# Reordering a linear-attention plus gated-MLP kernel behind its first gate block, with one batch's key features in 32-token tiles and one copy on ScalarE

## The chip, the cores and the metric

The kernel runs on one core of one Trainium2 chip. The metric is the device time of one execution in microseconds (us), the median over the runs shown; lower is better. The core has a matrix engine (TensorE, PE in the profile; its weight loads are shown apart as PEld), a vector engine (VectorE, DVE), an activation engine (ScalarE, ACT), a general engine (GpSimd, POOL) and a sync engine (SyncE, SP), which here only starts transfers (DMA). Each engine runs its own instructions strictly in the order in which the program wrote them.

## The reference

Four batches, four heads, 1088 tokens, 32 features a head. Queries and keys go through two 8x32 projections whose outer product gives 64 features; the attention is linear in them; its result x (1088 x 128 per batch) goes through a gated MLP in which the tokens are mixed by a 1088 x 1088 matrix:

```python
def phi(x):
    a = np.einsum('rd,bhsd->bhsr', S1, x)
    b = np.einsum('rd,bhsd->bhsr', S2, x)
    return np.einsum('bhsi,bhsj->bhsij', a, b).reshape(*x.shape[:-1], r * r)
q_p, k_p = (phi(q), phi(k))
kv = np.einsum('bhsf,bhsd->bhfd', k_p, v)
z = np.sum(k_p, axis=2)
num = np.einsum('bhsf,bhfd->bhsd', q_p, kv)
den = np.einsum('bhsf,bhf->bhs', q_p, z)[..., None] + 1e-06
...
h = gelu_tanh(x @ w_in)
u, v = (h[..., :d_ff // 2], h[..., d_ff // 2:])
v_n = (v - mean(v)) / np.sqrt(var(v) + 1e-06) * g_ln
v_s = np.einsum('ts,bsd->btd', w_sg, v_n) + b_sg[None, :, None]
gated = u * v_s
return (x + gated @ w_out)
```

Here d_ff is 1024, so v_n is 1088 x 512 for each batch, and the product with w_sg is the bulk of the work.

## The kernel before

Every large product keeps fp32 accuracy by splitting each operand into a high and a low part (`_h`, `_l`) and adding three products: high by high, high by low, low by high. In the token mixing these are the matmuls of lines 851 (`z_hi`, two a tile) and 860 (`z_lo`).

The 1088 tokens are cut into 9 tiles of 128 (the last half full) where they are contracted, and into three chunks of 362, 362 and 364 columns where they are the output. The 512 channels of v are four blocks of 128 (`db`). For each batch the stages are:

- `k1` (line 404): the keys of each token tile times the projections, into the PSUM tiles `pk`; `kb` (line 416, ScalarE) copies half of that; `features` (line 211, VectorE) makes the 64 products per head, `kp`; `k2` (line 436) contracts `kp` with v and a column of ones over the tokens, into `pkv`: 4 matmuls of 32 rows for each tile and pair of heads. `kv` (lines 447 and 448) copies `pkv` into `kv`, the second copy broadcasting the denominator's column to 32 columns.
- the same features for the queries (`qt`, `pab`, `ab`, `e_..`, `qph`, `qpl`: lines 469 to 529; they go through DRAM to be spread over partitions), then numerator and denominator (`pnd`, `den`), giving x and its split `x_h`, `x_l`.
- `unit`: `pu` (lines 875 to 877), three matmuls per block and chunk, then gelu on ScalarE, `u` (line 882). `pv` (lines 746 to 755), gelu `vn` (760), the layer norm's statistics (776 to 828), its split `vh` (838, ScalarE) and `vl` (843, VectorE).
- the token mixing `pz` (lines 851, 860) and then on VectorE `gt` = pz times gain plus bias (`scale`, line 888), times u (`gate`, line 895), split into `gh` (900, ScalarE) and `gl` (903, VectorE), and the output product `po` (lines 921 to 924), whose sum with x is stored.

PSUM has 8 banks, and every `pz`, `pu`, `po`, `pk`, `pkv` and so on takes the next of them (`bank`), so a matmul group that opens a bank waits until the last reader of that bank's earlier tile is done. Weights and inputs come by DMA; `w_l` are the low parts of w_sg, made on VectorE during batch 0.

Batch 3 does the mixing in another way (class `Fast`): sums of blocks of w_sg (`t1` to `t4`) are built in DRAM by transfers that GpSimd starts, loaded by `high` (line 1103, GpSimd's queue, into `wt_..h`) and by `load` (line 1096, SyncE, into `wr`), and `low` (line 1107, VectorE) subtracts to get `wt_..l`; the products are then those of lines 1012 to 1019, with tiles named `pz_(0, 'v')` and the like, and lines 1046 and 1050 for the third chunk.

The order of all this is written out by hand. Each piece is registered as a step by `at`, and a table `WHEN` of 1773 numbers gives each step its place; `Steps.run` sorts by it and emits the steps in that order, so the table sets the order on all engines at once:

```python
def run(self, tc):
    when = WHEN or range(len(self.steps))
    with tc.manual_schedule():
        for i in sorted(range(len(self.steps)), key=lambda i: (when[i], i)):
            self.steps[i][1]()
```

Of the kernel before, what the change touches and what calls it, by code (L numbers as in the profile page):

```python
# [15 lines left out]
B, H, S, D, R = 4, 4, 1088, 32, 8  # L16
P = 128
# [13 lines left out]
NARROW = 9  # L31
# [121 lines left out]
def tile_kernel(tc, qd, kd, vd, sd, wd, bd, wind, woutd, q0d, vid, outd, pool, dram, psum):  # L153
    nc = tc.nc
    mm = nc.tensor.matmul
    V, A, G = nc.vector, nc.scalar, nc.gpsimd
# [12 lines left out]
    T = {}  # L169
# [220 lines left out]
    class Attention:  # L390
# [9 lines left out]
        def k1(self, pk, t, i):  # L400
            k = T[f"k{self.b}"]
# [1017 lines left out]
```

## Time and profile before

| | |
|---|---|
| time, median of 3 runs (lowest to highest) | 322.85 us (322.66 to 323.17) |
| the profiled execution: its time / its span | 322.65 us / 320.9 us |
| TensorE busy, of the span | 312.4 us (97%) |
| VectorE busy | 273.2 us (85%) |
| ScalarE busy | 161.7 us (50%) |
| GpSimd busy | 35.0 us (11%) |
| mean granted TensorE clock | 0.997 |

The profile is of one execution. Its span runs from the first to the last instruction; 1.75 us of the execution's own time lie around it. A matmul record overlaps the next, so a matmul of 362 columns is shown with 0.32 us while a new one starts every 0.16 us; a loss on PE is therefore read from the starts.

### The profile page before, as it was taken

Reading aid. Unit: us, or ns where it says so; the run is one execution under the profiler, and the core shown is the slowest. Engines: PE = TensorE matmul, PEld = TensorE weight load, DVE = VectorE, ACT = ScalarE, POOL = GpSimd, SP = SyncE. Lnnn points to the kernel's source line nnn. Section 1 sums busy time; section 2 is a strip of 40 time slices with the busy share of each in tenths; the row PEclk is TensorE's granted clock in tenths of the full one; section 3 lists DMA queues with packets and bytes.
Section 4 is the critical chain, followed back from the end, with each engine's and each line's share of the span. In section 5 each row is a group of like instructions: output and inputs, shape, how many; then the busy total and the mean of one; then the engine's idle time right before and its main releaser. Section 6 shows DMA issues by size and latency. Waiting matters only on the chain.

```text
span 320.9 us, 6477 instructions
## 1 busy us (share of the span) xinstructions
PE 312.4 (97%) x2474; PEld 298.7 (93%) x2474; DVE 273.2 (85%) x660; ACT 161.7 (50%) x354; POOL 35.0 (11%) x52
## 2 busy tenths in 40 slices
PE   8999999899999999999999998999999999999995
PEld 6777999799999999999999997999999999999995
DVE  5999999999998968597988875598997889889865
ACT  4689814646549825354537930446345762433411
POOL 0300000024301100203400000333010000000000
PEclk9999999999999999999999999999999999999998
DMA  7999934764468625735160005684160022400002
GB/s 227 368 429 361 400 152 135 186 175 132 188 98 198 123 57 143 192 100 176 12 113 24 2 29 119 162 221 136 25 194 24 0 76 33 162 23 1 2 0 69
DMA packets 19774, 42.27 MB, mean 132 GB/s; under 512 B 2176, under 2 KB 14624, under 8 KB 19328
## 3 DMA queue, kind: packets, MB, share of 16 engines
q1 hardware_dynamic: 14784, 27.17, 27.5%
q0 software_dynamic: 4960, 14.70, 17.3%
q8 instruction: 19, 0.31, 0.4%
q14 instruction: 11, 0.09, 0.1%
HBM read 35.87 MB, written 8.94 MB: 140 GB/s over the span
## 4 chain that ended last, share of the span: by engine, by line
PE 79%; DVE 14%; issue 2%; ACT 2%; DMA 1%; SPq 1%; DVEq 0%; ACTq 0%
PE pz L851 28%; PE pz L860 12%; PE pz L1050 5%; DVE w_l L719 2%; PE pu L875 2%; PE pu L877 2%; PE pu L876 2%; PE pv L746 2%; PE pv L747 2%; PE pv L755 2%; PE po L924 2%; PE po L922 2%; PE po L921 2%; DMA vn<-in_q 1%; PE pkv L436 1%
## 5 line engine op out<-in xcount | busy, mean ns | idle before, releaser
L851 PE MATMUL pz<-w_h,vh 128*128 128x362 f32 (+1 forms) x324 | 105.4, 326 | 0.8 <-ACT u L882 0.8
L851 PE MATMUL pz<-w_h,vl 128*128 128x362 f32 (+1 forms) x324 | 105.2, 325 | 0.4 <-DVE vl L843 0.4
L860 PE MATMUL pz<-w_l,vh 128*128 128x362 f32 (+1 forms) x288 | 87.0, 324 | 0.0
L851 PEld LDWEIGHTS pz<-w_h,vh 128*128 128x128 f32 x324 | 60.8, 188 | 1.9 <-ACT u L882 1.1
L851 PEld LDWEIGHTS pz<-w_h,vl 128*128 128x128 f32 x324 | 60.8, 188 | 1.6 <-DVE vl L843 0.9
L860 PEld LDWEIGHTS pz<-w_l,vh 128*128 128x128 f32 x288 | 53.1, 188 | 0.1
L882 ACT ACTIVATE u<-pu 128x362 f32<-128x362 f32 (+1 forms) x48 | 22.6, 473 | 28.5 <-DVE gt L895 15.4
L900 ACT CAST gh<-gt 128x362 fp32r<-128x362 f32 (+1 forms) x47 | 22.7, 492 | 18.6 <-DVE gt L895 15.9
L888 DVE SCALAR_TENSOR_TENSOR gt<-pz,vi,b_bc 128x362 f32<-128x362 f32 (+3 forms) x41 | 23.6, 579 | 7.1 <-PE pz L851 6.3
L828 ACT ACTIVATE vn<-vn,nm,rs 128x512 f32<-128x512 f32 x36 | 28.1, 812 | 2.9 <-DVE nm L822 2.1
L903 DVE TENSOR_TENSOR gl<-gt,gh 128x362 fp32r<-128x362 f32 (+1 forms) x47 | 25.4, 547 | 2.6 <-ACT gh L900 2.0
L760 ACT ACTIVATE vn<-pv 128x512 f32<-128x512 f32 x36 | 21.0, 598 | 11.8 <-PE pv L755 11.0
L895 DVE TENSOR_TENSOR gt<-gt,u 128x362 f32<-128x362 f32 (+3 forms) x49 | 25.5, 525 | 0.8 <-ACT u L882 0.3
L776 DVE BATCH_NORM_STATS2 st<-vn 128x6 f32<-128x512 f32 x33 | 22.5, 683 | 3.9 <-ACT vn L760 3.2
L843 DVE TENSOR_TENSOR vl<-vn,vh 128x128 fp32r<-128x128 f32 (+1 forms) x54 | 22.2, 428 | 1.9 <-ACT vh L838 1.7
L550 DVE RECIPROCAL den<-den 128x362 f32<-128x362 f32 (+1 forms) x9 | 21.7, 2415 | 1.3 <-ACT den L545 1.2
L838 ACT CAST vh<-vn 128x128 fp32r<-128x128 f32 (+1 forms) x54 | 19.6, 403 | 6.2 <-PE pz L851 5.8
L1050 PE MATMUL pz<-w_h,wb 128*128 128x364 f32 x64 | 18.8, 324 | 0.0
L529 POOL TENSOR_TENSOR qpl<-e_0a,qph 128x362 fp32r<-128x362 f32 x6 | 6.3, 1056 | 109.9 <-ACT qph L524 83.9
L875 PE MATMUL pu<-x_h,win_h 128*128 128x362 f32 (+1 forms) x48 | 16.2, 337 | 0.0
L545 ACT ACTIVATE den<-pnd,mask 64x362 f32<-64x362 f32 (+1 forms) x18 | 10.1, 560 | 11.4 <-PE pnd L538 11.3
L876 PE MATMUL pu<-x_h,win_l 128*128 128x362 f32 (+1 forms) x48 | 15.7, 328 | 0.0
(330 smaller groups left out, 635.7 us busy)
## 6 DMA issues: line engine op xcount, KB each, us to landing
w_f<-in_w SPq DMA_DIRECT2D x9, 576.0 KB
wt<-in_w POOLq DMA_DIRECT2D x6, 768.0 KB, 7.7
w_h<-in_w POOLq DMA_DIRECT2D x2, 1152.0 KB, 8.5
vi<-in_v SPq DMA_DIRECT2D x7, 306.0 KB
w_h<-in_w POOLq DMA_DIRECT2D x1, 1728.0 KB, 14.5
k<-in_k SPq DMA_DIRECT2D x3, 576.0 KB
wt<-wt POOLq DMA_DIRECT2D x2, 768.0 KB, 6.8
out<-o SPq DMA_DIRECT2D x8, 181.0 KB
```

Source lines behind the costliest of these rows:

```text
L776: V.bn_stats(st, self.vn[:, t])
L828: A.activation(self.vn[:, t], self.vn[:, t], AF.Identity, bias=self.nm[:, t : t + 1], scale=self.rs[:, t : t + 1])
L843: V.tensor_sub(vl[:, ts], self.vn[:, ts, P * db : P * db + P], f32(vh[:, ts]))
L851: mm(self.z[db, ci], lhsT=self.parts[db][i][:, t], rhs=T["w_h"][:, t, AT[ci] : AT[ci] + cw], start=(t == 0 and i == 0), stop=(t == NT - 1 ...
L860: mm(self.z[db, ci], lhsT=self.parts[db][0][:, t], rhs=T["w_l", t][:, AT[ci] : AT[ci] + CH[ci][1]], start=False, stop=False,)
L875: mm(pu, lhsT=T["win_h"][:, ws], rhs=xh[:, cs], start=True, stop=False)
L882: A.activation(self.u[db, ci], self.pu.pop((db, ci)), AF.Gelu_apprx_tanh)
L888: V.scalar_tensor_tensor(self.gt[db, ci][:, s], self.z[db, ci][:, s], T["g_col"][:, db : db + 1], T["b_bc"][:, c0 : c0 + cw][:, s], op0=AL ...
L895: V.tensor_mul(gt, gt, self.u[db, ci][:, s])
L900: A.copy(self.g[db, ci][0], self.gt[db, ci])
L903: V.tensor_sub(self.g[db, ci][1], self.gt.pop((db, ci)), f32(self.g[db, ci][0]))
L1050: mm(self.z[db, ci], lhsT=w[:, i, t % 4], rhs=r[:, cs], start=(t == 0 and q == 0), stop=False)
```

## The change

The order of the first 339 steps, up to the end of batch 0's first gate block (about 46.7 us in the trace of before), stays. Behind it nearly every number of `WHEN` is new. Three more edits:

- `k1` works in tiles of 32 tokens instead of 64 for batch 1 (`D` is 32), so its 18 matmuls become 36 with half the output rows; the trace shows each fp32 matmul as two records. Batches 0, 2 and 3 stay.
- The copy of the denominators in `kv` (line 448) is issued on ScalarE instead of VectorE, in all batches, 2 a batch.
- `NARROW` goes; since it was 9 and t is below 9, `n` in `k2` is what it was.

```diff
-NARROW = 9
...
-    282, 284, 287, 291, 296, 293, 299, 304, 301, 309, 365, 103, 105, 109, 118, 130, 116, 137, 115, 142, 145, 153,
-    157, 166, 173, 182, 187, 192, 198, 201, 180, 275, 286, 360, 319, 328, 368, 371, 367, 223, 230, 264, 272, 305,
+    282, 284, 287, 291, 296, 293, 299, 304, 301, 309, 358, 103, 105, 109, 118, 130, 116, 137, 115, 142, 145, 153,
+    157, 166, 173, 182, 187, 192, 198, 201, 180, 275, 286, 360, 319, 328, 371, 485, 378, 223, 230, 264, 272, 305,
...
-            for r in range(0, P, 64):
+            n = D if self.b == 1 else 2 * D
+            for r in range(0, P, n):
                 mm(
-                    self.pk[t][r : r + 64], lhsT=k[:, P * t + r : P * t + r + 64], rhs=T["sk"][:, :64],
+                    self.pk[t][r : r + n], lhsT=k[:, P * t + r : P * t + r + n], rhs=T["sk"][:, :64],
                     start=True, stop=True, skip_group_check=True,
                 )
...
-            n = D if self.b or t >= NARROW else 2 * D
+            n = D if self.b else 2 * D
...
-                    V.tensor_copy(self.kvf[r, 1:3, c], self.pkv[r, :, D : D + 1].broadcast_to([64, 2, D]))
+                    A.copy(self.kvf[r, 1:3, c], self.pkv[r, :, D : D + 1].broadcast_to([64, 2, D]))
```

What the new numbers do is read from the instructions on each engine. A row is line, operation, out<-in and the shape; `pu_2_0` is block 2, chunk 0, and the last number of a name only counts tiles.

**TensorE, batch 0 and the k2 of batch 1, before.** The two units and the first mixing of block 2 (rows 245 to 253 of 1718; the k2 of batch 1 is in rows 233 to 235):

```order
L875 MATMUL pu_2_0_1014<-x_h,win_h 128x362
L876 MATMUL pu_2_0_1014<-x_h,win_l 128x362
L877 MATMUL pu_2_0_1014<-x_l,win_h 128x362
L875 MATMUL pu_2_1_1027<-x_h,win_h 128x362
L876 MATMUL pu_2_1_1027<-x_h,win_l 128x362
L877 MATMUL pu_2_1_1027<-x_l,win_h 128x362
L851 MATMUL pz_2_0_1034<-w_h,vh_2_885 128x362
L851 MATMUL pz_2_0_1034<-w_h,vl_2_886 128x362
L860 MATMUL pz_2_0_1034<-w_l_709,vh_2_885 128x362
```

**The same engine, after.** The units, the k2 (L436) and the first mixing of block 2 (rows 233 to 244 of 1719):

```order
L875 MATMUL pu_2_0_913<-x_h,win_h 128x362
L876 MATMUL pu_2_0_913<-x_h,win_l 128x362
L877 MATMUL pu_2_0_913<-x_l,win_h 128x362
L875 MATMUL pu_3_0_918<-x_h,win_h 128x362
L876 MATMUL pu_3_0_918<-x_h,win_l 128x362
L877 MATMUL pu_3_0_918<-x_l,win_h 128x362
L436 MATMUL pkv_927<-vi,kp_0_885 32x34 x24
L436 MATMUL pkv_927<-vi,kp_1_899 32x34 x24
L436 MATMUL pkv_927<-vi,kp_2_907 32x34 x24
L851 MATMUL pz_2_0_1002<-w_h,vh_2_814 128x362
L851 MATMUL pz_2_0_1002<-w_h,vl_2_815 128x362
L860 MATMUL pz_2_0_1002<-w_l_709,vh_2_814 128x362
```

The k2 of batch 1 has moved from in front of these units and of the six `po` matmuls between to a place directly ahead of the mixing of block 2, with a unit of block 3 ahead of it.

**TensorE, the k2 of batch 2, before.** What stands between the k1 of batch 2 (rows 596 and 597) and its k2; the last 9 rows and the k2 (rows 606 to 617):

```order
L921 MATMUL po_1_1804<-gh_0_1_1702,wout_h 128x362
L922 MATMUL po_1_1804<-gh_0_1_1702,wout_l 128x362
L924 MATMUL po_1_1804<-gl_0_1_1703,wout_h 128x362
L851 MATMUL pz_1_0_1720<-w_h,vh_1_1610 128x362
L851 MATMUL pz_1_0_1720<-w_h,vl_1_1611 128x362
L860 MATMUL pz_1_0_1720<-w_l_646,vh_1_1610 128x362
L851 MATMUL pz_1_0_1720<-w_h,vh_1_1610 128x362
L851 MATMUL pz_1_0_1720<-w_h,vl_1_1611 128x362
L860 MATMUL pz_1_0_1720<-w_l_666,vh_1_1610 128x362
L436 MATMUL pkv_1825<-vi,kp_0_1792 32x34 x24
L436 MATMUL pkv_1825<-vi,kp_1_1808 32x34 x24
L436 MATMUL pkv_1825<-vi,kp_2_1818 32x34 x24
```

**The same place, after.** The last 9 rows ahead of the k2, and the k2 (rows 565 to 576; its k1 is in rows 519 and 520):

```order
L860 MATMUL pz_0_0_1519<-w_l_735,vh_0_1478 128x362
L479 MATMUL pab_1_1719<-qt_1h,sk_76 128x362
L480 MATMUL pab_1_1719<-qt_1l,sk_75 128x362
L851 MATMUL pz_0_1_1598<-w_h,vh_0_1478 128x362
L851 MATMUL pz_0_1_1598<-w_h,vl_0_1479 128x362
L860 MATMUL pz_0_1_1598<-w_l_679,vh_0_1478 128x362
L851 MATMUL pz_0_0_1519<-w_h,vh_0_1478 128x362
L851 MATMUL pz_0_0_1519<-w_h,vl_0_1479 128x362
L860 MATMUL pz_0_0_1519<-w_l_679,vh_0_1478 128x362
L436 MATMUL pkv_1742<-vi,kp_0_1726 32x34 x24
L436 MATMUL pkv_1742<-vi,kp_1_1738 32x34 x24
L436 MATMUL pkv_1742<-vi,kp_2_1681 32x34 x24
```

Between the k1 and the k2 of batch 2 there were 17 matmuls, and there are 53 now. For batch 3 the k2 moves from row 1013 to row 939, which with the repeats in the rows and the weight loads makes about 77 fewer TensorE instructions ahead of it.

**VectorE, near the end, before.** The last low part of batch 3's weights, `wt_1l` (L1107), and the rows ahead of it (rows 554 to 565 of 624; the L1107 ahead of it is row 550):

```order
L895 TENSOR_TENSOR gt_0_0_3677<-gt_0_0_3677,u_0_0_3544 128x362
L979 TENSOR_TENSOR wb_0s_3699<-vn_3180,wb_0s_3699 128x512
L913 TENSOR_TENSOR x_f_3711<-x_h,x_l 128x364
L994 TENSOR_TENSOR vn_3180<-vn_3180 128x4x128
L888 SCALAR_TENSOR_TENSOR gt_0_2_3726<-pz_0_2_3466,vi,b_bc 128x364
L941 TENSOR_TENSOR o_2_3629<-o_2_3629,x_l 128x364
L903 TENSOR_TENSOR gl_0_0_3722<-gt_0_0_3677,gh_0_0_3721 128x362
L895 TENSOR_TENSOR gt_0_2_3726<-gt_0_2_3726,u_0_2_3731 128x364
L979 TENSOR_TENSOR wb_13_3751<-vn_3180,wb_13_3751 128x512
L986 TENSOR_TENSOR we_2_3705<-vn_3180,we_2_3705 128x128
L941 TENSOR_TENSOR o_1_3613<-o_1_3613,x_l 128x362
L1107 TENSOR_TENSOR wt_1l<-wr_3724,wt_1h 128x3x362
```

**The same place, after.** From the L1107 whose end frees the buffer `wr` of the load (rows 556 to 567 of 623):

```order
L1107 TENSOR_TENSOR wt_0l<-wr_3580,wt_0h 128x362
L1107 TENSOR_TENSOR wt_0l<-wr_3580,wt_0h 128x2x362
L1036 SCALAR_TENSOR_TENSOR vi<-pz_(0, 'w')_3619,vi 128x362
L895 TENSOR_TENSOR gt_2_2_3733<-gt_2_2_3733,u_2_2_3698 128x364
L908 TENSOR_TENSOR wout_f<-wout_h,wout_l 128x128
L1036 SCALAR_TENSOR_TENSOR gt_0_0_3789<-pz_(0, 'x')_3449,vi,b_bc 128x362
L979 TENSOR_TENSOR wb_0s_3752<-vn_3180,wb_0s_3752 128x512
L903 TENSOR_TENSOR gl_2_2_3784<-gt_2_2_3733,gh_2_2_3783 128x364
L1036 SCALAR_TENSOR_TENSOR gt_0_1_3797<-pz_(0, 'u')_3724,vi 128x362
L913 TENSOR_TENSOR x_f_3805<-x_h,x_l 128x362
L941 TENSOR_TENSOR o_2_3690<-o_2_3690,x_l 128x364
L1107 TENSOR_TENSOR wt_1l<-wr_3770,wt_1h 128x3x362
```

The two last L1107 stood 15 rows apart (rows 550 and 565) and now stand 10 apart (rows 557 and 567).

## Rows read from the trace of the kernel before

**Rows 1.** The page: busy time of each engine, and the chain by engine.
```profile
PE 312.4 (97%) x2474; PEld 298.7 (93%) x2474; DVE 273.2 (85%) x660; ACT 161.7 (50%) x354; POOL 35.0 (11%) x52
...
PE 79%; DVE 14%; issue 2%; ACT 2%; DMA 1%; SPq 1%; DVEq 0%; ACTq 0%
```

**Rows 2.** Windows: us, then busy us (instructions) of each engine, clock, DMA.
```profile
50.00:60.00 10.00, 9.62 (x221) 8.77 (x220) 9.81 (x24) 7.47 (x18) 0.00 (x0) 1.00 0.70 198
60.00:70.00 10.00, 9.22 (x53) 8.27 (x52) 9.83 (x24) 3.94 (x9) 1.68 (x2) 1.00 0.66 181
...
190.00:200.00 10.00, 8.57 (x215) 8.08 (x215) 6.12 (x18) 1.50 (x5) 0.00 (x0) 1.00 0.46 94
```

**Rows 3.** Waits of PE: engine line <- releaser: us, times, longest.
```profile
PE pkv L436 <- issue: 1.4, 1, 1.4
...
PE pz L851 <- ACT u L882: 0.8, 1, 0.8
...
PE pkv L436 <- ACT u L882: 0.4, 1, 0.4
```

**Rows 4.** Timeline of PE, 53 to 64 us: start, us, engine, line, operation [idle <-releaser].
```profile
53.43 1.27 PE L404 MATMUL pk<-sk,k 128*64 128x64 f32 x36
54.63 0.43 PE L875 MATMUL pu<-x_h,win_h 128*128 128x362 f32 x1
...
57.73 1.49 PE L436 MATMUL pkv<-vi,kp 128*32 128x34 f32 x144 [0.37 <-ACT u L882]
...
61.86 0.32 PE L877 MATMUL pu<-x_l,win_h 128*128 128x362 f32 x1
62.96 0.43 PE L851 MATMUL pz<-w_h,vh 128*128 128x362 f32 x1 [0.78 <-ACT u L882]
63.23 0.33 PE L851 MATMUL pz<-w_h,vl 128*128 128x362 f32 x1
```

**Rows 5.** Timeline of VectorE, 55 to 62 us.
```profile
55.50 3.06 DVE L211 TENSOR_TENSOR kp<-pk,kb 128x256 f32<-128x256 f32 x9
...
61.81 0.53 DVE L895 TENSOR_TENSOR gt<-gt,u 128x364 f32<-128x364 f32 x1
```

**Rows 6.** Timeline of ScalarE, 62 to 63 us.
```profile
62.43 0.47 ACT L882 ACTIVATE u<-pu 128x364 f32<-128x364 f32 x1 [2.72 <-DVE gt L895]
```

**Rows 7.** Timeline of PE, 125 to 128 us.
```profile
125.70 1.95 PE L436 MATMUL pkv<-vi,kp 128*32 128x34 f32 x144
```

**Rows 8.** Line 436: records with ns min/median/max, and the idle time before them.
```profile
L436 PE MATMUL pkv<-vi,vn x72: 224/224/245, 10.7 to 12.8; 128*64 128x34 f32 x72
...
  DVE kp L211: 0.2, 1
```

**Rows 9.** Timeline of PE, 194 to 198 us.
```profile
194.86 1.42 PE L436 MATMUL pkv<-vi,kp 128*32 128x34 f32 x136
197.71 0.27 PE L436 MATMUL pkv<-vi,kp 128*32 128x34 f32 x8 [1.43 <-issue]
```

**Rows 10.** Instruction queue in the page's part 3: packets, MB, share of 16 engines.
```profile
q8 instruction: 19, 0.31, 0.4%
```

**Rows 11.** The same queue between 195.2 and 196.5 us.
```profile
q8 instruction: 1, 0.02, 4.5%
```

**Rows 12.** Groups by line and shape: busy us, mean ns | idle before.
```profile
L448 DVE COPY kv<-pkv 64x64 f32<-64x64 f32 x6 | 1.3, 213 | 0.0
```

**Rows 13.** The same of ScalarE, its smallest copies.
```profile
L416 ACT COPY kb<-pk 128x32 f32<-128x32 f32 x3 | 0.6, 188 | 0.4 <-PE pk L404 0.4
```

**Rows 14.** Timeline of SyncE's queue, near 272 us.
```profile
272.17 0.32 SPq L1096 DMA_DIRECT2D wr<-wt  x1
```

**Rows 15.** Timeline of VectorE, near 281 us.
```profile
281.28 1.29 DVE L1107 TENSOR_TENSOR wt_1l<-wr,wt_1h 128x1086 fp32r<-128x1086 f32 x1
```

**Rows 16.** Timeline of PE, near 284 us.
```profile
283.83 0.32 PE L1013 MATMUL pz_(0, 'v')_3774<-wt_1l,wb 128*128 128x362 f32 x1
```

**Rows 17.** DMA issues between 270 and 282 us: KB, us to landing.
```profile
wt_1h<-wt POOLq DMA_DIRECT2D x1, 576.0 KB, 4.5
```

150 rows, old and new, of the table WHEN are left out of this document.

## The prediction

> **What bounds the kernel now.** I read the busy times and the chain first: TensorE is busy 312.4 of 320.9 us, and the chain that ended last is 79% PE [rows 1]. VectorE at 85% is next, but it waits for PE as often as PE for it. So the kernel is bound by TensorE's own instructions, and a new order that keeps all of them can only win what PE loses between them: 320.9 - 312.4 = 8.5 us at the most, of which the start and the tail, where the order stays or nearly stays, hold a large part. The granted clock is 1.00 (the 2.4 GHz level) in each of the windows [rows 2], so there is nothing to win in clock.
>
> Next come the windows of 10 us behind the point from which the order is new. Nearly all have PE at 10.00. Three do not: 9.62 at 50 to 60 us, 9.22 at 60 to 70 and 8.57 at 190 to 200 [rows 2]. The list of PE's waits names what ended them: 1.4 us of "issue" ahead of the k2 matmuls of line 436, 0.8 us of the token mixing for ScalarE's u, 0.4 us of k2 for u [rows 3]. The timelines place them: 0.37 us ahead of the k2 of batch 1 at 57.73, 0.78 us at 62.96 [rows 4], 1.43 us in the middle of the k2 of batch 3 at 197.71 [rows 9]. A fourth loss doesn't show as idle time in a window, since records overlap: the k2 of batch 2 takes 1.95 us for its 144 records [rows 7], that of batch 1 takes 1.49 for the same 144 [rows 4]; the 0.46 us between them is k2 going in pieces, as VectorE's features kp come just in time (the wait for kp under line 436 [rows 8]).
>
> **The change part by part.**
>
> *Batch 1, around 50 to 65 us.* The 0.78 us: the first mixing of block 2 opens a PSUM bank that u had to leave; u ran only from 62.43 for 0.47 us, after 2.72 us of idling for the gate product on VectorE [rows 6], and that product stood at 61.81 [rows 5], behind 3.06 us of features and the copies of kv. So the real cause is VectorE's backlog (9.81 and 9.83 busy of 10 in these two windows [rows 2]). In the new order two gate products of block 0 and the scaling of two more chunks come before the features, the output matmuls (`po`) between k2 and block 2's mixing are gone from there, and the k2 moves behind two units, directly ahead of block 2's mixing. From the features' 9 products of 3.06 / 9 = 0.34 us and PE's 0.16 us a matmul I place the k2 at about 57.8 us and the end of the last feature it needs at 58.5, with the k2 eating the 9 tiles in 1.4 us, so the last third is wanted at 58.8: slack 0.3 us, an estimate. The bank for block 2 is then free, since its u ran a block earlier. Removed: 0.37 + 0.78 = 1.15 us. What is late next if this slack is short is the same k2, at the price of the shortage.
>
> *k1 of batch 1.* The 36 records of 64-row tiles took 54.63 - 53.43 = 1.20 us, 33 ns each [rows 4]; there will be 72 records of 32-row tiles. No row of before has k1 in such tiles. The nearest is k2 in 32-row tiles, 1.49 / 144 = 10.3 ns a record [rows 4], against batch 0's in 64-row tiles, 2.1 / 72 = 29 ns [rows 8]: four narrow tiles work side by side. Lower bound: 72 x 10.3 ns = 0.74 us, -0.46. Upper bound: the price grows with the columns streamed (64 against 34), 0.74 x 64 / 34 = 1.40 us, +0.20. The ratio of the two k2 rows alone would give 1.20 x 20.6 / 29 = 0.85 us, -0.35. I take -0.20, between these, as k2's rows are the same kind of instruction but not the same width.
>
> The rows show a narrow tile's record at 10.3 ns. Against this speaks a rule of the Trainium skill, "TensorEngine Tiling (Array Packing)", section "Instruction Overhead": a matmul has a fixed overhead of about 60 cycles, and a dimension that is small already should not be tiled. By it 36 more records would cost 36 x 25 ns = 0.9 us more, an estimate from that page; by the rows above they cost a tenth of a microsecond or less. The rows decide, and that sum would be 1.1 us higher.
>
> *Batch 2.* Between k1 and k2 there were 17 matmuls, 2.8 us at 0.16 us each, in which VectorE had to make 3.06 us of features; now there are 53, some 8.5 us. So k2 finds them done: -0.46 us. VectorE has room there to be late by 5 us, so this is the safest of the terms.
>
> *Batch 3's 1.43 us.* PE stops after 136 of the 144 records for 1.43 us of "issue", that is, for nothing that an engine released [rows 9]. 136 matmuls and their 136 weight loads are 272 instructions. The instruction queue moved 19 packets [rows 10] for 2 x 2474 records [rows 1], so one packet carries some 260; and one of them lies exactly here, between 195.2 and 196.5 us [rows 11] (4.5% of 16 engines over 1.3 us is 0.94 us of transfer). I read it so: PE consumes instructions in blocks of some 256; the first border fell about 16 instructions into this k2, and the next was reached after only 1.4 us, while the block behind it took until 197.71, that is 2.8 us after the first border was passed at about 194.95. The k2 is the only place dense enough for this: elsewhere 260 instructions last 130 x 0.16 = 21 us. The new order has about 77 fewer instructions ahead of this k2, so the first border falls some 93 in and the next one 349 - 288 = 61 instructions behind its end. That is 195 instructions of k2 (1.0 us) and 30 matmuls (4.9 us), 5.9 us against 2.8 needed; even if the sequencer had passed the border 1.6 us (ten matmuls) before the array did, 4.4 are needed. So -1.43 us. For batch 1 the k1 is now 72 instructions longer; the same count puts one border 82 instructions into k1 and the next 160 into k2, with 16 full matmuls between: 0.5 + 2.6 + 0.8 = 3.9 us against 2.8 to 4.4. That costs between nothing and 0.5 us; I take nothing, and keep 0.5 for the range. For batch 2 the 53 matmuls between k1 and k2 lie between two borders.
>
> The skill's page "Runtime: NRT & Kernel Launch", section "Instruction fetch mechanics", speaks against my reading: blocks of 256 instructions agree with the 260 that the rows give, but it says that crossing such a border is mostly hidden. If it is so here, the 1.43 us are something else that need not go (the first rival).
>
> *The copy on ScalarE.* Six copies of 213 ns go from VectorE [rows 12]; ScalarE's small copies take 188 ns [rows 13] on an engine that is half idle [rows 1]. The kv's next reader waits for both, and they now run side by side: 0 on the path, between -0.3 and +0.3 us, if ScalarE is behind a gelu of 0.47 us [rows 6] at the time.
>
> *The rest of the order* moves steps that PE never waited for. I went through the transfers on SyncE's and GpSimd's queues and found one place with less room than before, in the last rival; I cost it at 0. The restart after a wait is lost too (0.27 us instead of 0.16 between the two starts behind 62.96 [rows 4], and a slot of 0.16 in the wait itself); I hold these 0.3 us against small new waits that I can't see.
>
> **Sum.** 322.65 (the profiled execution) - 0.37 - 0.78 - 0.20 - 0.46 - 1.43 = 319.41 us. The median of the runs is 0.20 above the profiled one, so 319.6.
>
> **Rivals.**
>
> 1. *The instruction stall stays*, in batch 3 or in another dense stretch, since its cause isn't the place of the border. For it: one stall is thin evidence, and one border must fall into each k2. Against: 272 is one block and 16, and the other k2s have none. 319.6 + 1.43 = 321.0.
> 2. *VectorE's backlog only moves.* It is 98% busy from 50 to 70 us [rows 2], and the new order takes only two copies a batch from it. If PE waits again for u or kp there, the 1.15 us and a part of k1's gain stay: 319.6 + 1.35 = 321.0; with the stall as well 322.4, no change. For it: VectorE's share. Against: the new order puts matmuls without readers on VectorE between its demands.
> 3. *The order does not do what it is written for*: the PE losses are the same by other names, 322.4 to 322.9.
> 4. *Slower: the last low weights come late.* Line 1107's `wt_1l` is read by PE at 283.83 [rows 16] and was made from 281.28 for 1.29 us [rows 15], from a load issued at 272.17 [rows 14]: 1.3 us of room behind the subtraction and 4 or more ahead of it. The new order lets the load start only when a VectorE instruction 10 rows earlier, instead of 15, has freed its buffer: I place this at about 276.3 us; with 4.5 us for a load of this size [rows 17] and 1.29 it is ready at 282.4, and PE wants it at about 283: room 0.6 us. Each microsecond beyond is a microsecond of PE. To be slower than before it must be late by 0.6 + 3.2 + 0.65 = 4.5 us, so the load would have to take twice its time, as with another such transfer in front of it: 324.
>
> **How the numbers follow.** A measurement of this kernel can tell about 0.2%, 0.65 us, from no change: below 322.2 is faster, above 323.5 slower. Forecast, 318.8 to 320.3: 0.60. One of rivals 1 and 2 alone, 320.3 to 321.7: 0.22. Both, or rival 3, about 322.2 to 323.2: 0.09. Rival 4: 0.06. Below 318.8, if the restarts and k1's lower bound come on top (319.6 - 0.3 - 0.26 - 0.3 = 318.7): 0.03. Faster: 0.60 + 0.22 + 0.03 = 0.85; same 0.09; slower 0.06. The range for 8 in 10 takes the forecast's bounds and rivals 1 and 2 alone: 318.7 to 321.4.
>
> **What would show it.** Right: no "issue" wait inside a k2; PE's windows from 50 to 70 us at 9.8 or more; the k2 of batch 2 at 1.5 us; batch 1's k1 at 0.75 to 1.4 us for 72 records. Wrong: new waits of `pz` or `pkv` for u, gt or kp near 55 to 80 us; an issue wait near 58 us in batch 1's k2; a wait of line 1013 for `wt_1l` near 280 us; or k1 above 1.4 us, with which narrow tiles have the price of the page and not of the rows.

## The result, and the profile after

The changed kernel takes 320.03 us (median of 6 runs, 318.73 to 320.43) against 323.01 us before (6 runs): a ratio of 0.9893, 95% interval 0.9860 to 0.9926. In a second set on another occasion it took 319.37 against 322.87, 0.9891 (0.9861 to 0.9921). Forecast: 319.6 us, 318.7 to 321.4.

The page of the changed kernel, busy times and the chain, which answer to [rows 1]:

```profile
PE 310.8 (98%) x2510; PEld 298.3 (94%) x2510; DVE 271.5 (85%) x654; ACT 163.0 (51%) x360; POOL 35.8 (11%) x52
...
PE 90%; DVE 6%; DMA 2%; SPq 1%; issue 0%; ACT 0%; DVEq 0%
```

PE's share of the chain went from 79% to 90%, "issue" from 2% to 0. PE's list of waits, whole, against [rows 3]:

```profile
PE warm L202 <- POOL ones L194: 0.9, 1, 0.9
PE pn L610 <- DMA vn<-in_q: 0.9, 1, 0.9
PE pk L404 <- DMA k<-in_k: 0.8, 2, 0.5
PE pz L851 <- DVE vl L843: 0.4, 1, 0.4
```

All three waits of [rows 3] are gone; what is left lies in the first 30 us, where the order is unchanged. The windows that had losses in [rows 2]:

```profile
50.00:60.00 10.00, 10.00 (x198) 9.37 (x199) 9.71 (x23) 5.94 (x14) 0.00 (x0) 1.00 0.59 135
60.00:70.00 10.00, 9.96 (x145) 9.81 (x133) 9.54 (x23) 4.51 (x11) 2.08 (x2) 1.00 0.54 123
...
180.00:190.00 10.00, 10.00 (x198) 9.73 (x197) 7.85 (x27) 8.31 (x20) 0.00 (x0) 1.00 0.39 109
190.00:200.00 10.00, 10.00 (x63) 10.00 (x62) 6.21 (x12) 1.79 (x4) 2.65 (x3) 1.00 0.60 130
```

And the dense stretches of PE: the k1 and k2 of batch 1, the k2 of batch 2 and that of batch 3 (which answer to [rows 4, 7, 9]):

```profile
55.40 1.21 PE L404 MATMUL pk<-sk,k 128*32 128x64 f32 x72
...
59.33 1.73 PE L436 MATMUL pkv<-vi,kp 128*32 128x34 f32 x144
...
118.08 1.49 PE L436 MATMUL pkv<-vi,kp 128*32 128x34 f32 x144
...
181.48 1.46 PE L436 MATMUL pkv<-vi,kp 128*32 128x34 f32 x144
```

**Three stretches.** To see where the time went, cut each execution at two records of PE that are the same instruction in every kernel: the 201st matmul record (near 15 to 17 us; the 211th and the 239th in the two kernels that begin with more small matmuls), and the first matmul behind the common 339 steps. The second one is the group that starts at 46.74 us in the trace of before:

```profile
46.74 1.47 PE L860 MATMUL pz<-w_l,vh 128*128 128x362 f32 x8
```

and at 48.09 us in the trace of after:

```profile
48.09 3.30 PE L860 MATMUL pz<-w_l,vh 128*128 128x364 f32 x19
```

From there to the end of the span it is 320.9 - 46.74 = 274.16 us before and 317.7 - 48.09 = 269.61 after: the part whose order is new gained 4.55 us (the spans are printed to 0.1 us, so such a stretch is good to 0.05), more than the 3.24 of my sum. But the median gained only 3.0 to 3.5. The stretch ahead of it, in which no step was moved on PE, VectorE or ScalarE, had become longer: 48.09 - 16.01 = 32.08 us from the 201st record, against 46.74 - 15.18 = 31.56 before. A possible reason, which experiment 4 tests, stands on GpSimd. Before:

```profile
78.26 1.50 POOL L1082 DMA_DIRECT2D wt<-in_w  x2
```

After:

```profile
23.93 0.75 POOL L1082 DMA_DIRECT2D wt<-in_w  x1 [0.18 <-issue]
```

This is the 768 KB copy that begins batch 3's sum t1. It started 54 us earlier, among the loads of batch 0's weights.

### The profile page after: what moved, and what is told of

It is laid out like the page before. It is cut to its first block, busy times and chain, and to the rows that moved or that the text cites. A ratio compares the mean times of both kernels' runs of the same rounds, so it can differ in the third digit from the quotient of the medians.

```text
span 317.7 us, 6545 instructions
## 1 busy us (share of the span) xinstructions
PE 310.8 (98%) x2510; PEld 298.3 (94%) x2510; DVE 271.5 (85%) x654; ACT 163.0 (51%) x360; POOL 35.8 (11%) x52
## 4 chain that ended last, share of the span: by engine, by line
PE 90%; DVE 6%; DMA 2%; SPq 1%; issue 0%; ACT 0%; DVEq 0%
PE pz L851 33%; PE pz L860 15%; PE pz L1050 5%; PE pu L875 3%; PE pu L877 2%; PE pu L876 2%; PE pv L755 2%; PE pv L747 2%; PE pv L746 2%; PE po L924 2%; PE po L921 2%; PE po L922 2%; DMA vn<-in_q 2%; PE pkv L436 1%; PE pk L404 1%; PE pnd L537 1%
## 5 line engine op out<-in xcount | busy, mean ns | idle before, releaser
L903 DVE TENSOR_TENSOR gl<-gt,gh 128x362 fp32r<-128x362 f32 (+1 forms) x47 | 24.5, 529 | 3.3 <-PE po L922 1.7
L838 ACT CAST vh<-vn 128x128 fp32r<-128x128 f32 (+1 forms) x54 | 20.4, 404 | 8.1 <-PE pz L851 7.7
L877 PE MATMUL pu<-x_l,win_h 128*128 128x362 f32 (+1 forms) x48 | 15.7, 327 | 0.0
```

What stands on the lines that cost most here:

```text
L903: V.tensor_sub(self.g[db, ci][1], self.gt.pop((db, ci)), f32(self.g[db, ci][0]))
```

## The experiments

The table holds each profiled execution: the two stretches (201st record to the common point; common point to the end of the span), where a k2 of batches 1 to 3 stopped for nothing an engine released (batch, after how many of 144 records, start-to-start distance there), and the median over the runs. The first 15 us vary by 2 us between executions, as the first loads land earlier or later (the 201st record lies between 15.15 and 17.25 us), so stretches say more than totals.

| kernel | early stretch | rest | stop in k2 | median us (runs) |
|---|---|---|---|---|
| before | 31.56 | 274.16 | batch 3, 136: 1.63 us | 323.01 (6) |
| after | 32.08 | 269.61 | batch 1, 80: 0.24 | 320.03 (6) |
| after_again | 31.55 | 269.50 | batch 1, 80: 0.08 | 319.37 (6) |
| after_k1_64 | 33.22 | 269.46 | none | 320.09 (4) |
| after_copy_on_dve | 32.55 | 269.86 | batch 1, 80: 0.47 | 320.68 (8) |
| before_k1_32 | 31.57 | 273.73 | none | 323.11 (10) |
| order_from_batch2 | 31.56 | 282.59 | batch 1, 64: 0.11 | 331.10 (4) |
| before_t1_early | 34.04 | 274.07 | batch 3, 136: 1.70 | 323.85 (10) |
| after_t1_late | 31.58 | 269.70 | batch 1, 80: 0.24 | 318.81 (5) |
| after_t1_late_k1_64 | 31.60 | 269.63 | batch 1, 116: 0.17 | 319.20 (6) |
| before_warm19 | 31.58 | 273.90 | none | 322.89 (1) |
| after_warm33 | 31.55 | 269.45 | none | 319.79 (1) |

**1. The stop in k2: is it the border of an instruction block?** First, batch 1's k1 in wide tiles again, in the changed kernel.

```diff
-            n = D if self.b == 1 else 2 * D
+            n = 2 * D
```

> The changed kernel, but with batch 1's k1 in 64-row tiles as before (36 records instead of 72; 72 fewer TensorE instructions ahead of everything behind it). In the trace of the changed kernel the 72 narrow records took 1.21 us where the 36 wide ones took 1.20, and its k2 of batch 1 lost 0.235 us after its 80th matmul, that is 160 instructions in. If that small stop is the border of an instruction block, it moves to 232 instructions in (after the 116th matmul) and its size changes, to nothing if the sequencer ran ahead in the wide k1, to at most about 1.5 us if it did not; nothing moves at the 80th. If it is a wait for data or for a bank, it stays at the 80th. k1 itself: 1.2 us in both theories, so the narrow tiles neither gain the 0.20 us of the prediction nor cost the page's 0.9. Time within 0.3 us of the changed kernel if the stop goes, 1.3 slower if it grows.

Measured: 320.09 us (ratio to before 0.9900, 0.9869 to 0.9931), the same as the changed kernel. The two dense groups of batch 1:

```profile
56.70 1.27 PE L404 MATMUL pk<-sk,k 128*64 128x64 f32 x36
...
60.73 1.49 PE L436 MATMUL pkv<-vi,kp 128*32 128x34 f32 x144
```

The stop after the 80th record is gone (1.49 us instead of 1.73), with k2, its data and its place among the steps unchanged. Narrow or wide, k1 takes nearly the same: 1.14 us from its first start to the next group's in the changed kernel, 1.20 here.

Then the opposite: the kernel before, with nothing changed but the narrow k1.

```diff
-            for r in range(0, P, 64):
+            n = D if self.b == 1 else 2 * D
+            for r in range(0, P, n):
```

> The kernel before, with its order and its copies, but with batch 1's k1 in 32-row tiles: 72 more TensorE instructions ahead of batches 2 and 3, and no step moved. If the stop of 1.43 us (1.62 between starts) in batch 3's k2 comes from the border of an instruction block, it goes: the border moves from 16 instructions into that k2 to 56 ahead of it, so the next lies 200 in, with 28 more full matmuls (4.5 us) to fetch in. Then the time is about 1.6 us below before, without any new order. If the stop belongs to the order of batch 3 (a wait that the profile does not show), it stays and the time is that of before.

Measured: 323.11 us, before 323.12 on the same chip (0.9993, 0.9972 to 1.0014). The k2 of batch 3 ran through:

```profile
196.87 1.49 PE L432 MATMUL pkv<-vi,kp 128*32 128x34 f32 x144
```

So a change of 72 instructions in batch 1 removes a stop in batch 3, 140 us later. That speaks for the block border. But the 1.6 us did not come with it: the rest fell only from 274.16 to 273.73. PE's list of waits has two new entries, both some 12 us behind this k2:

```profile
PE pnd L532 <- ACT qph L520: 0.3, 1, 0.3
PE pu L871 <- DVE gt L884: 0.2, 1, 0.2
```

With their restarts and a third such gap, the distances between starts from 208 to 227 us exceed the usual slots by 0.47 + 0.08 + 0.33 + 0.11 + 0.16 + 0.11 = 1.26 us, which is the 1.63 us of the stop less the 0.4 that was gained. Behind the stop in the kernel before, only its restart of 0.11 us exceeds the slots in the same stretch. So in the old order the stop covered work that was late anyway; in the new order these waits do not appear.

The same with another way to shift the instructions: 5 more of the small matmuls at the start (20 instructions).

```diff
-WARM = 14
+WARM = 19
```

> The kernel before with 5 more of the small matmuls that warm TensorE at the start (19 instead of 14), 20 more instructions of TensorE ahead of everything, nothing moved. If the stop in batch 3's k2 is the border of an instruction block, it moves by 20 instructions, 10 matmuls: after the 126th record instead of the 136th; its length is at most the 1.62 us between starts. If it is a wait for a tile or a transfer, it stays after the 136th. The time, beside about 0.5 us more at the start, is that of before.

Measured: 322.89 us (before 323.62 beside it, one run each). The stop is not at the 136th record and not at the 126th: it is absent, and the waits of line 536 for qph (0.4 us) and of line 875 for gt (0.2) stand in its place, as in the run above:

```profile
195.32 1.49 PE L436 MATMUL pkv<-vi,kp 128*32 128x34 f32 x144
```

A shift of 20 instructions puts the border, by the prediction's count, 4 instructions ahead of this k2 instead of 16 into it, so it now lies on the other side of the wait at which TensorE's sequencer (the part that issues its instructions) stood for kp. The first weight load of this k2 shows that wait, before:

```profile
194.86 1.31 PEld L436 LDWEIGHTS pkv<-vi,kp 128*32 128x32 f32 x136 [0.23 <-DVE kp L211]
```

The last experiment of this kind gives the changed kernel the old place of the border in batch 3, with 19 more small matmuls (76 instructions).

```diff
-WARM = 14
+WARM = 33
```

> The changed kernel with 19 more of the small matmuls at the start (33), 76 more instructions of TensorE ahead of everything, so that the k2 of batch 3 has the block border 16 instructions in again, as it had before. If the place of the border is all that counts, the stop of 1.4 to 1.6 us is there again after the 136th record. If the sequencer also has to have been held up ahead of k2 (before, it waited for the features kp until just ahead of this k2; in the new order kp is ready some microseconds earlier), it fetches the next block in time and the stop is below 0.5 us. The start costs some 2 us more in both.

Measured: 319.79 us (one run), no stop:

```profile
181.75 1.49 PE L436 MATMUL pkv<-vi,kp 128*32 128x34 f32 x144
```

Here the features were ready earlier, and the first weight load of k2 was released by no engine (the idle 0.23 us stand there all the same):

```profile
181.75 1.37 PEld L436 LDWEIGHTS pkv<-vi,kp 128*32 128x32 f32 x144 [0.23 <-issue]
```

So the place alone is not enough. The instruction queue shows when the block was fetched. Its one packet of that time starts between 195.4 and 195.5 us in the kernel before, 0.56 us after the start of k2; between 193.3 and 193.4 in before_warm19, 2.0 us ahead of k2; between 180.6 and 180.7 in after_warm33, 1.14 us ahead of k2. The queue's line for these three windows of 0.1 us (packets, MB, share of 16 engines; 58.5% of 16 x 0.1 us is 0.94 us of transfer):

```profile
q8 instruction: 1, 0.02, 58.5%
...
q8 instruction: 1, 0.02, 58.0%
...
q8 instruction: 1, 0.02, 57.4%
```

And the end of each stop follows a packet: after the 136th record (two executions), the 80th (four) and the 116th (one), PE resumes 2.2 to 2.8 us after the packet's start, 1.28 to 1.50 us after its end (before: packet 195.42 to 196.36, PE again at 197.71; after: 57.95 to 58.89, again at 60.27). So PE stops when it reaches the block's first instruction before the block is there. That the wait for kp is what made the fetch late in the kernel before fits the three times above, but was not varied alone; why the fetch of batch 1's block came only 1.2 to 1.5 us ahead of k2 in the new order stays open.

The place in the instruction stream is shown too: the stop is after the 136th record in two kernels with the same count ahead, after the 80th in all four executions of the new order with a narrow k1 and the same count ahead, and after the 116th in one of the two with a wide k1, which is 72 instructions (36 records) later; it goes with a shift of 20, 72 or 76. The 0.11 us after the 64th record in order_from_batch2 does not fit this count and stays unexplained.

**2. Batch 1's part, or batches 2 and 3?** The order of before for the first 530 steps, up to the copies of kv of batch 1, and the new order for the rest; the narrow k1 and the copies on ScalarE undone.

```diff
-steps 530 to 1772: sorted by the WHEN of before
+steps 530 to 1772: sorted by the WHEN of after
```

> The order of before up to the copies of batch 1's kv (the first 530 steps), the new order for all other steps; k1 of batch 1 in 64-row tiles and the copies of the denominators on VectorE as before. If the gain of batch 1's part comes from the order there, PE's losses between 50 and 77 us come back (2.2 us against the changed kernel), and those of batches 2 and 3 stay away (0.46 and 1.62 us less than before): about 2.1 us below before, 0.9 or so above the changed kernel's median allowing for the seam. If VectorE's backlog was relieved by the copies on ScalarE or the narrow k1 instead, much of the loss at 57 and 62 us shows the same with either order.

Measured: 331.10 us (1.0267), far slower, for a reason of its own: at the seam.

```profile
PE pu L871 <- DVE den L550: 5.1, 1, 5.1
PE pv L742 <- DVE den L550: 1.3, 1, 1.3
...
PE pz L847 <- ACT u L878: 0.8, 1, 0.8
PE pkv L432 <- ACT u L878: 0.4, 1, 0.4
```

The two waits for `den` come from joining the orders; the total says nothing. What can be read is that the 0.8 and 0.4 us of batch 1 are back with the old order there (the 201st record and the common point lie as in before, so with the same loads), and that the stops of batches 2 and 3 stay away. This run undoes the small edits together with batch 1's order, so by itself it does not tell them apart. The runs that change one of them alone do: the new order has none of these waits with the wide k1 (after_k1_64) or with the copies on VectorE (after_copy_on_dve), and the old order keeps both with the narrow k1 (before_k1_32). So the order removed them, not the small edits.

**3. The copies on ScalarE.**

```diff
-                    A.copy(self.kvf[r, 1:3, c], self.pkv[r, :, D : D + 1].broadcast_to([64, 2, D]))
+                    V.tensor_copy(self.kvf[r, 1:3, c], self.pkv[r, :, D : D + 1].broadcast_to([64, 2, D]))
```

> The changed kernel, with the copies of the denominators on VectorE as before. In the trace of the changed kernel the four copies of a batch go one after the other over two engines, VectorE waiting 0.27 us for ScalarE's copy in the middle; the group takes 0.95 us instead of 0.72. Nothing of it is on PE's path, so the time is that of the changed kernel (0 within 0.3 us) and VectorE's four copies take 0.72 us. If VectorE's backlog of batch 1 is so tight that 0.4 us count, PE waits again near 62 to 66 us and the time rises by up to 0.4.

Measured: 320.68 us (0.9930, 0.9903 to 0.9958), not to be told from the changed kernel. Its rest is 0.25 us longer, and its stop in k2 is 0.47 us instead of 0.24, which is that difference. In the changed kernel the copies alternate, on VectorE:

```profile
62.50 0.21 DVE L447 COPY kv<-pkv 64x64 f32<-64x64 f32 x1
62.98 0.23 DVE L447 COPY kv<-pkv 64x64 f32<-64x64 f32 x1 [0.27 <-ACT kv L448]
```

and on ScalarE:

```profile
62.74 0.21 ACT L448 COPY kv<-pkv 64x64 f32<-64x64 f32 x1 [3.32 <-DVE kv L447]
63.24 0.21 ACT L448 COPY kv<-pkv 64x64 f32<-64x64 f32 x1 [0.29 <-DVE kv L447]
```

Each waits for the one before (all four read one PSUM tile and write one tile; no run tells which of the two orders them): 62.50 to 63.45, 0.95 us, where four copies on VectorE alone take 0.73. VectorE is freed of 0.4 us and idles 0.27 of them. No wait of PE shows any of this.

**4. The early transfer.** The changed kernel as it is, with the one step moved back, with that and the wide k1, and the kernel before with the one step moved forward, side by side. The first has no edit.

> The changed kernel as it is, beside the three others of this call. From the 200th matmul record of TensorE (near 16 us) to the first matmul behind the common 339 steps its profile took 32.08 us, where three kernels with the order of before took 31.56 each; behind that point it took 269.6 us, before 274.2. If the early loss comes from the transfer of 768 KB that GpSimd now starts at 23.9 us instead of 78.3, this stretch is above 31.8 us again. Time 320.0.

The step moved back, in GpSimd's order:

```diff
 L444 MEMSET kv_1006 128x256
-L1082 DMA wt_1056<-in_w 512x1x384
 L529 ISA
 L529 TENSOR_TENSOR qpl_1_1070<-e_0a,qph_1_1069 128x362
 L529 TENSOR_TENSOR qpl_0_1096<-e_0a,qph_0_1095 128x362
 L529 TENSOR_TENSOR qpl_2_1158<-e_1a,qph_2_1157 128x362
 L529 TENSOR_TENSOR qpl_3_1202<-e_1a,qph_3_1201 128x362
+L1082 DMA wt_1056<-in_w 512x1x384
 L529 TENSOR_TENSOR qpl_4_1302<-e_2a,qph_4_1301 128x364
```

> The changed kernel with one step moved: the copy that begins batch 3's sum t1 (line 1082, 768 KB from the weights, GpSimd's queue) again behind the fourth low part of batch 1's query features, where it starts near 78 us, instead of ahead of the first, where GpSimd has nothing to wait for and starts it at 23.9 us among the loads of batch 0's weights. If that transfer is what delays the loads of w_f and of the output weights (the last four w_f loads took 5.1 to 5.8 us to issue instead of 2.9), the stretch from the 200th matmul record to the common point is 31.56 us again, ScalarE's and VectorE's waits for the output weights near 38 us go, and the time falls by 0.5 to 1.6 us, to 318.5 to 319.5. If the early loss is chance (when the first loads land), nothing changes: 320.0. If the sum t1 is then late for batch 3, PE waits for line 1012 or 1013 and the time rises.

The same, and the wide k1 of experiment 1:

```diff
-            n = D if self.b == 1 else 2 * D
+            n = 2 * D
```

> The kernel of after_t1_late, also with batch 1's k1 in 64-row tiles. The stop after the 80th matmul of batch 1's k2 (0.235 us, and 0.46 in another run) should be absent, as in after_k1_64: 0.2 to 0.4 us below after_t1_late, if the instruction block explains it; the same time if not. It should beat both kernels: 318.3 to 319.2 us.

The kernel before, with the same copy put ahead of batch 1's first qpl:

```diff
 L444 MEMSET kv_992 128x256
+L1082 DMA wt_1295<-in_w 512x1x384
 L529 ISA
...
 L529 TENSOR_TENSOR qpl_3_1200<-e_1a,qph_3_1199 128x362
-L1082 DMA wt_1295<-in_w 512x1x384
 L1082 DMA wt_1297<-in_w 512x1x384
```

> The kernel before with the one step moved the other way: the copy for t1 ahead of batch 1's first low part of the query features, so GpSimd starts it near 23 us. If this transfer among batch 0's weight loads is the price, the stretch from the 200th matmul record to the common point grows from 31.56 us to 32.1 to 33.2 and the time by 0.5 to 1.6 us, to about 324. If it costs nothing, 323.1 as before.

Measured: with the copy late the early stretch is 31.56, 31.57, 31.56, 31.58, 31.60 and 31.58 us in six kernels. With it early it is 32.08, 31.55, 33.22, 32.55, 34.04 and 31.55. after_t1_late takes 318.81 us, all five runs within 318.69 to 318.94 (ratio 0.9865, 0.9840 to 0.9890); after_again, on the same chip, 319.37 with runs from 318.70 to 321.36, so its best runs are as fast. How much of its other runs is the transfer is not shown: its profiled execution, 320.09 us, has no early loss, but reached its 201st record only at 17.25 us. The early copy in the kernel before makes that 0.31% slower (1.0031, 1.0010 to 1.0051): 323.85 against 322.87. So the price in the early stretch varies from execution to execution, from nothing to 2.5 us. Its way to PE, in before_t1_early: SyncE takes 5.66 us to issue the last four loads of w_f, as against 2.90 in the kernel before (shown first),

```profile
27.32 2.90 SPq L301 DMA_DIRECT2D w_f<-in_w  x4
...
28.49 5.66 SPq L297 DMA_DIRECT2D w_f<-in_w  x4
```

the output weights land late for ScalarE,

```profile
39.57 0.66 ACT L238 ACTIVATE woa<-raw_out 128x512 f32<-128x512 f32 x1 [3.61 <-DMA raw_out<-in_w_out]
```

and VectorE, which must prepare them ahead of the next `w_l` and `vl`, waits 2.22 us for that,

```profile
40.27 0.43 DVE L239 TENSOR_SCALAR wot<-woa 128x512 int32<-128x512 int32 x1 [2.22 <-ACT woa L238]
```

so that PE waits for vh and vl:

```profile
41.33 0.43 PE L847 MATMUL pz<-w_h,vh 128*128 128x362 f32 x1 [0.51 <-ACT vh L834]
42.17 0.44 PE L847 MATMUL pz<-w_h,vl 128*128 128x362 f32 x1 [0.41 <-DVE vl L839]
```

In after_t1_late the four loads are issued in 2.83 us and ScalarE has no wait there:

```profile
27.65 2.83 SPq L296 DMA_DIRECT2D w_f<-in_w  x4
```

The slow issue alone does not make the loss: in after_again the four loads took 4.92 us, and the early stretch lost nothing. What decides is not shown.

after_t1_late is the fastest of these kernels: 0.6 us below the changed one by medians, though their intervals against before overlap. The wide k1 added nothing that can be measured (319.20 us; the rest differs by 0.07 us): its stop moved from the 80th to the 116th record instead of going.

## Why the prediction held, point by point

- **PE-bound, and only PE's own losses can be won.** Right. VectorE stays at 9.71 and 9.54 of 10 us between 50 and 70, and yet PE has no wait there: the second rival is out, for the order alone decides what the same VectorE work delays.
- **Batch 1, -1.15 us.** Mechanism right, size too small. Summing over all starts from 46 to 80 us what exceeds the usual slot of their shape by over 0.06 us gives some 3.1 us before and 1.0 after: -2.1. The step that failed is that I took idle times as the loss: 0.37 and 0.78 us of idling are 0.53 and 0.94 between starts, and restarts and small gaps of 0.07 to 0.17 us, which no list of waits shows, went from 1.6 us to 0.7.
- **Batch 2, -0.46.** Right: 1.95 us to 1.49. The wait for kp in [rows 8], which I cited for it, is however that of batch 3's first weight load.
- **Batch 3, -1.43.** Right in effect, -1.62 between starts. My reason was half of it. The stop is the wait for a block, but I counted the fetch from the moment the array passes the border, and the packets show that it can start 2.0 us ahead of k2 or 0.56 us behind its start (after_warm33 has the old place and no stop). And in the old order removing the stop was worth only 0.3 to 0.4 us (273.73 and 273.90 against 274.16). That the new order cashed all of it is not shown by a run; it follows from the sum, since 2.1 for batch 1, 0.46 and 1.62 make 4.2 of the 4.55 us. The Trainium skill's page "Runtime: NRT & Kernel Launch", section "Instruction fetch mechanics", calls the crossing of such a border mostly hidden. The trace agrees for 18 of 19 blocks of before; the exceptions cost 1.63 us in that kernel and 0.08 to 0.47 in the changed one and its variants.
- **Batch 1's k2, nothing to 0.5 us for its border, taken as nothing.** It cost 0.24 us, exactly 160 instructions in, as counted. This is, in small, the issue wait that I had named as a sign of being wrong.
- **k1, -0.20.** The size was wrong by 0.14: counted as in the prediction, from first start to the next group's, 56.54 - 55.40 = 1.14 us for 72 records against 1.20 for 36, so -0.06. That is 15.8 ns a record, where I had bounds of 10.3 and 19.4 and took a value between the scaling by columns and the plain ratio; the scaling by columns was the better neighbour. The rule of the Trainium skill, "TensorEngine Tiling (Array Packing)", section "Instruction Overhead", of about 60 cycles for each matmul would have made 72 x 25 ns = 1.8 us of it, an estimate from that page; the trace does not agree.
- **Copies on ScalarE, 0 on the path.** Right, but they don't run side by side, as I had written.
- **"I went through the transfers on SyncE's and GpSimd's queues ... I cost it at 0."** This step failed. I checked whether the moved transfers come late, and not what they collide with when they come early. Moved ahead of the GpSimd instructions that had stood before it, this one started as soon as GpSimd was free; here 54 us earlier. It cost 0 to 2.5 us an execution in the early stretch.
- **Rival 4** (the last low weights late) did not come. The load of `wt_1l` was issued at 275.31 us (I had put its release at 276.3), line 1107 ran from 280.78 for 1.29 us, and PE read it at 283.10: 1.0 us of room instead of 0.6.

That the sum came out so near the median is partly luck: 1.3 us too little gain in the part with the new order met the early loss that I had not seen (0.5 us in the profiled execution) and first loads that landed 0.8 us later there. With the copy late the same order takes 318.81 us, at the low edge of the range.

## What to carry to other kernels

When steps are reordered by a table, follow each moved DMA on its own queue in both directions: what held it there before, how early it can start without that, and which loads it then meets. Count a stop of TensorE from start to start, with its restart, and not by the idle time that the profile prints. And before a stop is priced as a gain, look at what is late just behind it: removing the same 1.6 us was worth 0.3 to 0.4 in the old order, and by the sum nearly all in the new one.

## What the runs showed of the hardware

- A dense run of small matmuls (288 instructions in 1.5 us) can outrun TensorE's instruction queue: it cost 1.63 us in the kernel before, and shifting the stream by 20 instructions at the very start of the program removes it. In seven executions with such a stop PE resumed 1.28 to 1.50 us after the end of an instruction packet.
- In order_from_batch2, PE stood idle for 5.06 us and came back at half the clock: granted 0.50 (the 1.2 GHz level) from 99 to 104.5 us, with starts 0.30 us apart instead of 0.16, and 0.99 behind that. Its timeline and windows (columns as in [rows 2]):

```profile
98.82 0.64 PE L871 MATMUL pu<-x_h,win_h 128*128 128x362 f32 x1 [5.06 <-DVE den L550]
99.25 0.51 PE L872 MATMUL pu<-x_h,win_l 128*128 128x362 f32 x1
99.55 0.51 PE L873 MATMUL pu<-x_l,win_h 128*128 128x362 f32 x1
```

```profile
99.00:104.50 5.50, 5.50 (x19) 5.50 (x20) 2.06 (x10) 1.25 (x3) 0.47 (x1) 0.50 0.41 72
104.50:110.00 5.50, 5.50 (x34) 5.44 (x33) 0.59 (x1) 1.50 (x4) 0.05 (x1) 0.99 0.45 146
```

So a stop of 5 us cost nearly 8, by an estimate: 19 matmuls in that window at 0.14 us more each are 2.7 us on top.
